# Laying the false arms of two run-time tests next in the program of an attention and expert kernel

## The chip, the core and the metric

The kernel runs on one core of a Trainium2 chip. The metric is the device time of one execution in microseconds (us). Each of the core's engines has a program of its own: TensorE (PE; its weight loads are shown apart as PEld), VectorE (DVE), ScalarE (ACT), GpSimd (POOL) and SyncE (SP), the last of which here does nothing but start transfers and read numbers into registers. They meet through semaphores. A run-time test stands in all five programs: each engine reads the number into a register of its own and branches by itself.

## The reference, cut to what matters

Three stages follow each other on 1536 tokens of width 512: attention with a local window and block summaries, a dense layer of three weight matrices with a maximum, and an expert layer. Only the last matters here:

```
skip_score = x @ w_skip
do_compute = skip_score > 0
out = x.copy()
xc = x[do_compute]
logits = xc @ w_gate
e_idx = np.argmax(logits, axis=1)
... gate_w: the softmax probability of the chosen expert
for e in range(E):                       # 8 experts
    mask = e_idx == e
    h = np.maximum(xc[mask] @ w1[e], 0.0)
    y[mask] = gate_w[mask, None] * (h @ w2[e])
out[do_compute] = xc + y
```

How many tokens go to which expert is known only when the program runs, so the number of token tiles (128 tokens each) per expert is a number in a register, and the program branches on it.

## The kernel before, in words

The attention stage and the dense layer are one long straight program, written out by hand-made planning (`arrange`), and fill the first 297 us. While they end, the counts of tokens per expert are taken (`guess`, `plan`), and written as small integers to the tile `ints`. Matrix products are made of three TensorE passes each, on a high and a low part of either factor (the `h` and `l` in `wh`, `wl`, `xth`, `xtl`).

The expert stage then goes through token tiles. `pair(p, t)` works on two tiles (256 tokens) of the expert whose weights lie in buffer set p: `first(f)` multiplies into `ph` banks (L1111), ACT and DVE make `hth` and `htl` of it (L1114, L1115), `second(f)` multiplies into `py` (L1123, shown as pm), and `end(2)` adds and scatters the rows to `out` (DVE L1086, POOL L1089). In the middle, `next_x` prepares `xth`, `xtl` for the next pair (ACT L738, DVE L739). `single(p, t)` works on one tile: its first products are at L1204, the Relu at L1206, the turning of the hidden values at L1210 to L1212, the second products at L1246. With `dense=True` it works on the last 128 rows of the whole token list in their place, reads those rows of `out` back (SP, L1181), does its last products at L1176 in two halves, and writes the rows (DVE L1185, SP L1186).

`pair` and `single` begin with `begin`: POOL copies the indices and the rows of the tiles (L1070, L1072). Nothing that PE does in its first products reads them; DVE's last addition does.

The order of the expert stage is set by nested tests. After two pairs a test at L1349 (others to do than the common case) leads to `most`, and there:

- two pairs more, then L1325: are there more than 5 tiles left for the biggest expert? If so, another pair, then
- L1327: more than 7? If so, yet another pair. Then `odd()`, which is written out in each arm:
- L1319: is the count odd? If so a single tile. Then `last()`, written out in each arm again:
- L1311: is there a `DENSE` mark? If so, `single` for the second expert and `single` with `dense=True`.

With the inputs here the test of L1325 holds, L1327 and L1319 do not, and L1311 does: the profile shows five pairs (40 ACT instructions of L1114, 8 for each pair), then one single tile and the dense one. So one arm of each of the four tests is run, and the program ends.

Where an arm lies in the program is a matter of its own. `preferred_fallthrough_block=True` puts the true arm right behind the test and the false arm far away; `False` puts the false arm right behind it. Without the argument the true arm lies next. The arm that lies far away is reached by a jump, in all five programs.

Of the kernel before, what the change touches and what calls it, by code (L numbers as in the profile page):

```python
# [43 lines left out]
ONES, DENSE, OTHER = 32, 64, 128  # L44
# [102 lines left out]
def build(tc, a, out):  # L147
# [571 lines left out]
    def reg(t, hi, **kw):  # L719
        return nc.values_load(t, min_val=0, max_val=hi, skip_runtime_bounds_check_because=why, **kw)  # L720
# [34 lines left out]
    def raw_load(c, e):  # L755
        nc.sync.dma_start(M2["raw"][c], chunk_src(c, e))
# [110 lines left out]
    for n, (j, f) in enumerate(ws):  # L867
        t, w = 19.7 + 4.25 * n, (j, f)
# [8 lines left out]
    for f in range(FT1):  # L877
        t, w = 24.7 + 4.25 * ws.index((3, f)), (3, f)
# [143 lines left out]
    def tail_i(row):  # L1022
        nc.sync.dma_start(mi, table[bass.ds(row, TAIL), :].unsqueeze(0).broadcast_to([4, TAIL, 2]))
# [275 lines left out]
    def most(w):  # L1299

        b0, b1, l0 = (reg(ints[:, i * NE + k:i * NE + k + 1], 14, **SP) for i, k in ((2, 0), (2, 1), (3, 0)))
        MR[1], MR[2] = (reg(ints[:, 5 * NE + k:5 * NE + k + 1], NROW - P, **SP) for k in (1, 2))
        e2 = reg(ints[:, NE + 2:NE + 3], NE - 1, **SP)
        pair(0, b0 + 1, 1)
        tail_i(MR[2])
        for c in range(NCH):
            raw_load(c, e2)
        pair(0, b0 + 2, FAST2)

        def last():  # L1310
            with tc.If((w & DENSE) > 0, preferred_fallthrough_block=True) as dense:  # L1311
                single(1, b1 + 1, last=True, hr=M2["raw"], then=True)
                single(0, 0, last=True, hr=M2["raw"][2:], dense=True)
            with dense.Else():
                with tc.If((w & ONES) > 0):
                    single(1, b1 + 1, last=True, hr=M2["raw"])

        def odd():
            with tc.If((w & 1) > 0) as one:  # L1319
                single(0, l0, hr=M2["raw"])  # L1320
                last()
            with one.Else():
                last()

        with tc.If((w & (ONES - 1)) > 5, preferred_fallthrough_block=True) as four:  # L1325
            pair(0, b0 + 3)
            with tc.If((w & (ONES - 1)) > 7, preferred_fallthrough_block=True) as five:  # L1327
                pair(0, b0 + 4)
                odd()
            with five.Else():  # L1330
                odd()
        with four.Else():
            odd()
# [9 lines left out]
    with tc.If(EA > EARLY, preferred_fallthrough_block=True) as early2:  # L1343
        with tc.manual_schedule():
            pair(0, 0, gen=steps())
            numbers()
            pair(0, 1)
            word = reg(ints[:, 6 * NE:], 2 * OTHER - 1)
            with tc.If(word >= OTHER, preferred_fallthrough_block=False) as others:  # L1349
                any_ranks()  # L1350
            with others.Else():
                most(word)
# [78 lines left out]
```

## Time and profile before

| what | us |
|---|---|
| median of three runs (460.86 to 462.88) | 462.82 |
| the profiled execution, its own time | 464.36 |
| its span, from first to last instruction | 462.6 |
| PE busy in the span | 434.4 (94%) |
| DVE, ACT, POOL busy | 248.8, 197.6, 127.9 |
| attention and dense layer | 0 to 297 |
| five pairs | 297 to 423.6 |
| single tile, dense tile, end | 423.6 to 462.6 |

To be read so: a busy PE is the engine that sets the pace nearly everywhere, and a stretch in which it stands still is time of the whole kernel unless another engine is late as well. "issue" in a wait or in the chain of waits is time in which an engine waited for nothing that the profile shows. [...]

### The profile page before, as it was taken

Reading aid. Unit: us, or ns where it says so; the run is one execution under the profiler, and the core shown is the slowest. Engines: PE = TensorE matmul, PEld = TensorE weight load, DVE = VectorE, ACT = ScalarE, POOL = GpSimd, SP = SyncE. Lnnn points to the kernel's source line nnn. Section 1 sums busy time; section 2 is a strip of 40 time slices with the busy share of each in tenths; the row PEclk is TensorE's granted clock in tenths of the full one; section 3 lists DMA queues with packets and bytes.
Section 4 is the critical chain, followed back from the end, with each engine's and each line's share of the span. In section 5 each row is a group of like instructions: output and inputs, shape, how many; then the busy total and the mean of one; then the engine's idle time right before and its main releaser. Section 6 shows DMA issues by size and latency. Waiting matters only on the chain.

```text
span 462.6 us, 9488 instructions
## 1 busy us (share of the span) xinstructions
PE 434.4 (94%) x3446; PEld 390.4 (84%) x3450; DVE 248.8 (54%) x787; ACT 197.6 (43%) x522; POOL 127.9 (28%) x177
## 2 busy tenths in 40 slices
PE   7977979999999999999999999999999999996895
PEld 3556769999999899989999988998999798895775
DVE  4887999989963353445114174587147631313021
ACT  2799987755464482356211173211116412111111
POOL 2232453233112440433102511142323123322100
PEclk9998989999999999999999999999999999999799
DMA  8993644567525265220030290312941570011001
GB/s 237 256 303 112 221 151 143 183 228 233 201 84 189 93 182 132 39 86 27 3 117 21 52 350 12 137 10 82 331 129 46 169 264 27 28 48 28 28 28 50
DMA packets 28173, 58.51 MB, mean 126 GB/s; under 512 B 6163, under 2 KB 8723, under 8 KB 28104
## 3 DMA queue, kind: packets, MB, share of 16 engines
q1 hardware_dynamic: 25544, 51.71, 35.3%
q0 software_dynamic: 2560, 5.96, 4.1%
q8 instruction: 33, 0.54, 0.5%
q14 instruction: 36, 0.29, 0.2%
HBM read 48.16 MB, written 10.47 MB: 127 GB/s over the span
## 4 chain that ended last, share of the span: by engine, by line
PE 70%; DVE 9%; DMA 6%; issue 5%; ACT 5%; POOL 2%; SPq 1%; POOLq 0%; ACTq 0%
PE pm L368 19%; PE ph L1111 13%; PE pm L1123 12%; PE pm L395 11%; PE ph L1204 3%; ACT pr L278 3%; DMA raw<-in_m 3%; DMA raw<-in_kt 2%; PE pt L293 2%; PE po L306 2%; PE sc L259 2%; DVE cx L349 1%; PE pm L1176 1%; PE ptx L731 1%; DVE cx L353 1%
## 5 line engine op out<-in xcount | busy, mean ns | idle before, releaser
L368 PE MATMUL pm<-xh,wh 128*128 128x384 f32 x288 | 67.0, 352 | 2.5 <-DVE t L377 1.3
L368 PE MATMUL pm<-xl,wh 128*128 128x384 f32 x288 | 62.8, 337 | 0.0
L368 PE MATMUL pm<-xh,wl 128*128 128x384 f32 x288 | 62.6, 336 | 0.0
L368 PEld LDWEIGHTS pm<-xh,wh 128*128 128x128 f32 x288 | 50.3, 192 | 4.8 <-DVE t L377 1.9
L1114 ACT ACTIVATE hth<-ph 128x256 fp32r<-128x256 f32 x40 | 15.4, 386 | 88.8 <-PE ph L1111 85.5
L368 PEld LDWEIGHTS pm<-xl,wh 128*128 128x128 f32 x288 | 51.8, 189 | 0.0
L368 PEld LDWEIGHTS pm<-xh,wl 128*128 128x128 f32 x288 | 51.3, 188 | 0.3 <-DVE wl L361 0.3
L1115 DVE SCALAR_TENSOR_TENSOR htl<-ph,hth 128x256 fp32r<-128x256 f32 x40 | 16.8, 422 | 57.1 <-ACT hth L1114 57.1
L377 DVE TENSOR_TENSOR t<-pm,t 128x384 f32<-128x384 f32 x48 | 26.5, 553 | 37.8 <-PE pm L368 36.9
L288 POOL TENSOR_TENSOR pr<-pr,se 128x360 f32<-128x360 f32 x32 | 26.2, 824 | 68.9 <-DVE se L284 48.0
L395 PE MATMUL pm<-wh,h 128*128 128x262 f32 (+1 forms) x288 | 42.7, 287 | 1.3 <-ACT v L215 1.1
L278 ACT ACTIVATE pr<-pr,mx 128x120 f32<-128x120 f32 x96 | 36.7, 386 | 10.6 <-DVE mx L272 10.5
L385 POOL TENSOR_TENSOR h<-t,h 128x384 fp32r<-128x384 f32 x24 | 26.1, 1093 | 49.1 <-ACT h L382 47.6
L395 PEld LDWEIGHTS pm<-wh,h 128*128 128x128 f32 x288 | 37.9, 189 | 2.1 <-ACT v L215 1.3
L1123 PE MATMUL pm<-wh,hth 128*128 128x512 f32 x80 | 31.8, 397 | 0.0
L1123 PE MATMUL pm<-wh,htl 128*128 128x512 f32 x80 | 31.4, 393 | 0.0
L1123 PE MATMUL pm<-wl,hth 128*128 128x512 f32 x80 | 31.3, 392 | 0.0
L343 POOL TENSOR_SCALAR cx<-cx 128x512 f32<-128x512 f32 x24 | 18.3, 762 | 37.0 <-ACT cx L335 33.3
L562 POOL DMA_INDIRECT table<-rtab,rsi x12 | 12.0, 997 | 59.7 <-DVE rsi L553 25.3
L744 POOL DMA_INDIRECT xn<-x2d,inx x14 | 14.9, 1065 | 46.8 <-DVE xm L1077 31.1
L382 ACT CAST h<-t 128x384 fp32r<-128x384 f32 x24 | 11.9, 513 | 35.2 <-DVE t L377 33.8
L1111 PE MATMUL ph<-xth,wh 128*128 128x256 f32 x160 | 26.4, 286 | 0.0
(342 smaller groups left out, 871.2 us busy)
## 6 DMA issues: line engine op xcount, KB each, us to landing
raw<-in_m SPq DMA_DIRECT2D x48, 256.0 KB, 4.7
raw<-in_wx SPq DMA_DIRECT2D x22, 512.0 KB, 4.3
kx<-in_kx SPq DMA_DIRECT2D x12, 360.0 KB, 3.8
vx<-in_vx SPq DMA_DIRECT2D x14, 288.0 KB, 3.8
qt<-in_qt SPq DMA_DIRECT2D x16, 192.0 KB, 5.8
x2d<-raw SPq DMA_DIRECT2D x12, 256.0 KB, 4.7
raw<-in_kt SPq DMA_DIRECT2D x7, 384.0 KB, 9.4
raw<-in_vt SPq DMA_DIRECT2D x7, 384.0 KB, 5.0
```

Of the source, the lines that this page charges most:

```text
L278: nc.scalar.activation(pr[:, t, :], pr[:, t, :], AF.Exp, bias=mx[:, t:t + 1], scale=-1.0, accum_out=se[:, t:t + 1])
L288: nc.gpsimd.tensor_tensor(pr, pr, se.unsqueeze(2).broadcast_to([P, TPG, KT]), ALU.mult)
L343: nc.gpsimd.tensor_scalar(x, x, HIGH, LOW, ALU.min, ALU.max)
L368: nc.tensor.matmul(ST["ch", u, f, j], l[j, f][:, c * P:(c + 1) * P], r[u][:, c, :], start=(cs[0] == 0 and n == 0), stop=(cs[-1] == KC1 - 1 ...
L377: nc.vector.tensor_tensor(ST["t1", u, f], ps, ST["t1", u, f], ALU.max)
L385: nc.gpsimd.tensor_tensor(HL[u, f], ST["t1", u, f], HH[u, f].bitcast(F32), ALU.subtract)
L395: nc.tensor.matmul(ps, l[u, f][:, t * P:(t + 1) * P], r[3, f][:, lo:hi], start=(part != 1 and n == 0), stop=(part != 0 and n == len(ops) - 1))
L744: nc.gpsimd.indirect_dma_start(out=xn[t], out_offset=None, in_=x2d, in_offset=bass.IndirectOffsetOnAxis(ap=inx[:, t, 0:1], axis=0), bounds ...
L1111: nc.tensor.matmul(ps, w[:, o:o + P], r[:, d, :], start=(n == 0), stop=(n == 3 * KC1 - 1))
L1114: nc.scalar.activation(hh, ps, AF.Relu)
L1115: nc.vector.scalar_tensor_tensor(hl, ps, 0.0, hh.bitcast(F32), ALU.max, ALU.subtract)
L1123: nc.tensor.matmul(py[i], l[:, o:o + P], r, start=(f == 0 and n == 0), stop=(f == 7 and n == 2))
```

## The change

Two tests in `most` get the argument that lays their false arms right behind them. No instruction is added or removed on any engine, and no wait: the two far arms and the two near ones change their places.

```
         def odd():
-            with tc.If((w & 1) > 0) as one:
+            with tc.If((w & 1) > 0, preferred_fallthrough_block=False) as one:
                 single(0, l0, hr=M2["raw"])
                 last()
             with one.Else():
...
             pair(0, b0 + 3)
-            with tc.If((w & (ONES - 1)) > 7, preferred_fallthrough_block=True) as five:
+            with tc.If((w & (ONES - 1)) > 7, preferred_fallthrough_block=False) as five:
                 pair(0, b0 + 4)
                 odd()
             with five.Else():
```

On PE, in the program before, the test of L1327 stands behind the last product of the fifth pair, and behind the test lies a sixth pair:

```order
L1123 MATMUL pm_4026<-wl0_5_3718,hth1_4022 128x512
L1123 MATMUL pm_4026<-wh0_5_3717,htl1_4024 128x512
L1327 REGISTER_ALU
L1327 COMPARE_AND_BRANCH
L1111 MATMUL ph0_3500<-xth_3509,wh0_0_3564 128x256
L1111 MATMUL ph0_3500<-xth_3509,wh2_0_3574 128x256
```

The false arm of it, the test of L1319, is about 10,000 rows further on, behind the arms for all other cases; behind that test lies a single tile, and the arm that is run, with the test of L1311, lies 236 rows behind it:

```order
L1315 UNCONDITIONAL_BRANCH x2
L1319 REGISTER_ALU
L1319 COMPARE_AND_BRANCH
L1204 MATMUL ph0_3500<-wh0_0_3564,xth_3509 128x512
L1204 MATMUL ph0_3500<-wl0_0_3565,xth_3509 128x512
...
L1311 REGISTER_ALU
L1311 COMPARE_AND_BRANCH
L1204 MATMUL ph0_3500<-wh1_5_3952,xth_3509 128x512
L1204 MATMUL ph0_3500<-wl1_5_3953,xth_3509 128x512
```

So two jumps are taken, at L1327 and at L1319, and none at L1311. On PE, in the program now, the three tests and the arm that is run stand in one piece:

```order
L1123 MATMUL pm_4026<-wl0_5_3718,hth1_4022 128x512
L1123 MATMUL pm_4026<-wh0_5_3717,htl1_4024 128x512
L1327 REGISTER_ALU
L1327 COMPARE_AND_BRANCH
L1319 REGISTER_ALU
L1319 COMPARE_AND_BRANCH
L1311 REGISTER_ALU
L1311 COMPARE_AND_BRANCH
L1204 MATMUL ph0_3500<-wh1_5_3952,xth_3509 128x512
L1204 MATMUL ph0_3500<-wl1_5_3953,xth_3509 128x512
L1204 MATMUL ph0_3500<-wh1_5_3952,xtl_3510 128x512
```

The product on `wh1_5` that came last in the far arm is now the third test's neighbour, and the sixth pair has gone to the far end. The programs of DVE, ACT, POOL and SP move in the same way. The jump from the end of the arm to the end of the program is there in both.

## Rows read from the trace of the kernel before

**Rows 1.** Page, busy time: us (share of the span) and instructions of each engine.

```profile
PE 434.4 (94%) x3446; PEld 390.4 (84%) x3450; DVE 248.8 (54%) x787; ACT 197.6 (43%) x522; POOL 127.9 (28%) x177
```

**Rows 2.** Chain of waits from 415 us on: start us, us, what.

```profile
423.65 5.58 issue
429.23 6.39 PE ph L1204 x18
```

**Rows 3.** Timeline, PE: start us, us, engine line, operation, tiles, count, [idle before].

```profile
423.26 0.39 PE L1123 MATMUL pm<-wh,htl 128*128 128x512 f32 x1
429.23 0.76 PE L1204 MATMUL ph<-wh,xth 128*128 128x512 f32 x1 [5.58 <-issue]
...
435.46 0.60 PE L1210 MATMUL ph<-ident,raw 128*128 128x128 f32 x4
```

**Rows 4.** Timeline, PE, the dense tile: the same eighteen products and turning.

```profile
444.75 0.39 PE L1204 MATMUL ph<-wh,xth 128*128 128x512 f32 x1
...
448.97 0.60 PE L1210 MATMUL ph<-ident,raw 128*128 128x128 f32 x4
```

**Rows 5.** Windows, PE: from:to and length us, busy (instructions), granted clock, DMA share, GB/s.

```profile
296.00:423.60 127.60, 127.59 (x967) 1.00 0.35 110
425.00:426.00 1.00, 0.00 (x0) 1.00 0.09 16
427.00:428.00 1.00, 0.00 (x0) 0.50 0.09 20
431.00:433.20 2.20, 2.20 (x6) 0.50 0.33 123
434.00:437.40 3.40, 3.40 (x18) 1.00 0.01 2
```

**Rows 6.** DMA queues, 423.6 to 426 us: packets, MB, share.

```profile
q8 instruction: 2, 0.03, 7.8%
```

**Rows 7.** Waits, 422 to 463 us: us in total, times, longest.

```profile
POOL ic L1070 <- issue: 4.0, 1, 4.0
```

**Rows 8.** Timeline around the tests of L1349 (344 us) and L1325 (400 us, POOL 408 us).

```profile
343.93 0.39 PE L1123 MATMUL pm<-wh,htl 128*128 128x512 f32 x1
344.16 0.66 PE L1111 MATMUL ph<-xth,wh 128*128 128x256 f32 x4
...
399.97 0.53 PEld L1111 LDWEIGHTS ph<-xth,wh 128*128 128x128 f32 x4 [0.20 <-issue]
...
407.33 0.97 POOL L1089 DMA_INDIRECT out<-yo,isc  x1 [2.56 <-DMA out<-yo,isc]
...
408.30 0.20 POOL L1070 COPY ic<-im 128x4 int32<-128x4 int32 x1
```

**Rows 9.** Timeline, DVE and POOL from 421 us on.

```profile
421.02 1.28 DVE L739 TENSOR_TENSOR xtl<-ptx,xth 128x512 fp32r<-128x512 f32 x2
423.01 1.43 DVE L1086 SCALAR_TENSOR_TENSOR yo<-pm,ic,xr 128x512 f32<-128x512 f32 x2 [0.70 <-PE pm L1123]
424.56 1.04 POOL L1089 DMA_INDIRECT out<-yo,isc  x1 [0.37 <-POOL isc L1087]
429.58 1.00 POOL L1089 DMA_INDIRECT out<-yo,isc  x1 [3.97 <-DMA out<-yo,isc]
434.68 0.61 POOL L1072 COPY xr<-xm 128x512 f32<-128x512 f32 x1
445.01 0.75 DVE L1086 SCALAR_TENSOR_TENSOR yo<-pm,ic,xr 128x512 f32<-128x512 f32 x1 [2.88 <-PE pm L1246]
446.58 0.99 POOL L1089 DMA_INDIRECT out<-yo,isc  x1 [11.16 <-DVE yo L1086]
```

**Rows 10.** Timeline, the end: SP's transfers and DVE's addition before the last.

```profile
449.45 0.35 SPq L1181 DMA_DIRECT2D xr<-out  x1
...
455.78 0.48 DVE L1185 SCALAR_TENSOR_TENSOR yo<-pm,mo,xr 128x256 f32<-128x256 f32 x1 [1.56 <-PE pm L1176]
...
457.72 0.34 SPq L1186 DMA_DIRECT2D out<-yo  x1
```

More of the change, by code (lines that the diff above doesn't have):

```diff
@@ L1318, in odd @@
         def odd():
-            with tc.If((w & 1) > 0) as one:
+            with tc.If((w & 1) > 0, preferred_fallthrough_block=False) as one:
                 single(0, l0, hr=M2["raw"])
@@ L1326, in most @@
             pair(0, b0 + 3)
-            with tc.If((w & (ONES - 1)) > 7, preferred_fallthrough_block=True) as five:
+            with tc.If((w & (ONES - 1)) > 7, preferred_fallthrough_block=False) as five:
                 pair(0, b0 + 4)
```

## The prediction, made before the changed kernel was run

> **What bounds the kernel now.** I read the page's busy times first: PE works in 94% of the span [rows 1], so the question is where the other 6% lie and whether one of them is at a test. The chain of waits answers it. It runs along PE from the fifth pair into the single tile, and between them stands one piece of 5.58 us that belongs to nobody: "issue", time in which PE waited for no other engine and no transfer that the trace shows [rows 2]. The timeline of PE shows the same hole from the other side: the last product of the fifth pair starts at 423.26, the first of the single tile at 429.23 [rows 3]. These two stand on either side of the tests of L1327 and L1319, which are both false here and both jump. In the hole, two packets of a queue that carries instructions move, 0.03 MB [rows 6], so PE's program itself was being brought in. POOL, which passes the same tests later, shows a hole of its own of 4.0 us right there [rows 7].
>
> The second thing to see is the clock. It is 1.00 through the pairs, still 1.00 at 425 to 426, and 0.50 at 427 to 428, after PE has stood still for some 3 us; the products that follow run at 0.50 until about 433.4, and at 434 it is 1.00 again [rows 5]. So the hole costs twice: while PE stands, and in the first products behind it.
>
> **The change, part by part.** Nothing is added to any engine's work. Two taken jumps become two that are not taken, on five engines. What matters is PE.
>
> 1. The hole. Within the fifth pair and in the dense tile one 512-wide product follows the other by 0.23 us: eighteen products from 444.75 to the turning at 448.97 take 4.22 us, 0.234 each [rows 4]. Without jumps the first product of the single tile would start 0.23 after 423.26, at 423.49. It started at 429.23. This is 5.74 us.
>
> 2. The clock. From the first product of the single tile to its first turning, the same eighteen products take 435.46 - 429.23 = 6.23 us [rows 3], where the dense tile takes 4.22 at clock 1.00 [rows 4]. The excess is 2.01 us. If PE never stands, the clock has no cause to fall: at clock 1.00 the pairs ran without a pause, 127.59 us of 127.6 [rows 5]. I count all of it as gained.
>
> 3. What tests cost that do not jump. Before already shows two such: L1349, whose false arm lies next, and L1325, whose true arm does. At L1349 the next product starts 0.23 us after the one before, as if there were no test; at L1325, which follows 64 short products, the weight load stands idle for 0.20 us; on POOL the next instruction after L1325 starts at 408.30, where the one before ends [rows 8]. The three tests now stand together on PE. Their cost lies between nothing (the seam of L1349, which like this one follows long products, behind which PE's program can run ahead) and 3 x 0.20 = 0.60 us. I take nothing, from the nearest row, and keep 0.6 for the range. It cannot be below nothing, since the same three tests are passed before.
>
> [...]
>
> 4. What could be late next. The single tile's first products need `xth` and `xtl`; DVE has made the latter at 421.02 + 1.28 = 422.30, 1.2 us before 423.49. The second products write the bank that DVE's addition reads until 424.44 [rows 9], and come 4.22 us and more behind the first, after 427.7. DVE's addition at the end of the single tile, at 445.01, would come 7.75 us earlier, at 437.26. It needs the rows that POOL copies until 434.68 + 0.61 = 435.29: already early enough by 2.0 us if POOL gained nothing, and POOL's own hole of 4.0 us goes as well. The scatter of the single tile, at 446.58, would come at 438.83; POOL has its predecessor off at 430.58, and the longest time that a scatter made the next wait here is 429.58 - 424.56 = 5.02 us, so it is free by 434.6 [rows 9]. The rows that SP reads back at 449.45 are needed by DVE at 455.78 [rows 10]; both move with the scatter and with PE, by the same amount. So the holes of DVE, ACT, POOL and SP are covered and worth nothing, and PE's are worth all.
>
> 5. The end. After SP's last transfer is issued at 457.72 + 0.34 = 458.06 [rows 10], the span goes on to 462.6. The jump to the program's end is in both programs, far away in both. I count no change.
>
> The sum: 5.74 + 2.01 = 7.75 us, less 0 to 0.6. The profiled execution's own time is 464.36, so it would be 456.61; that execution is 1.54 us over the median of the runs, 462.82. Against the median: 462.82 - 7.75 = 455.07, taken as 455.1.
>
> **The rivals.**
>
> One stall stays. The hole is the price of two jumps; I do not know from the trace how it divides. If code behind three tests in a row, or the first stretch of the new arm, is still brought in late once, PE would stand for half the hole, 5.74 / 2 = 2.87 us. That is shorter than the 3 us or so after which the clock fell, so the second gain stays whole: 7.75 - 2.87 = 4.88, or 457.9. For it: instruction packets move in the hole, so fetching is slow enough to be seen. Against it: PE ran from 296 to 423.6 through two such tests and four seams between pairs without a stall [rows 5, 8].
>
> Nothing changes. Either the hole is not the price of the jumps but of testing (three tests, 1.9 us each, taken or not), or the places in the program do not survive to the chip. Then 462.8. Against it: two tests that are not taken show 0 and 0.20 us [rows 8].
>
> PE without a rest loses its clock: the slower side. In the program before, the pause at 423.65 is the one rest PE has between 296 us and the end. If the clock were then lowered later, at the dense tile, its products from 444.75 to about 457.2, 12.4 us at 1.00, would take twice that. The price is 12.4 us at most, and it decides from 7.75 us of lost time on; in full it gives 462.82 - 7.75 + 12.4 = 467.5. Against it: 127.6 us of unbroken work with the clock at 1.00 go before, and the one fall of it in this stretch came after PE had stood still, not after it had worked [rows 5].
>
> **How the numbers follow.** Full gain 0.80, its own range 453.4 to 456.6 (0.6 for the tests, and some 1.5 us either way for the spread of 2.0 us that the three runs of before show). One stall stays 0.12 (457.9). Nothing changes 0.05 (462.8). The clock is lost later 0.03 (467.5). The likeliest is 455.1. A range from 453.3 to 458.3 holds nearly all of the first two cases and leaves out the others. Faster by over 0.5% (2.3 us, about what a measurement of this kernel can tell from no change) are the first two cases: 0.92. Same 0.05, slower 0.03.
>
> **What would show it.** In the profile after: no piece "issue" of more than 0.6 us in the chain at the fifth pair's end; the first product of L1204 less than 1 us behind the last of L1123; granted clock 1.00 from there to the end of the dense tile; eighteen products to the first turning in 4.2 us; POOL's hole before L1070 gone; all from 429 on earlier by 7 to 8 us, with an end as long as before, some 4.5 us behind SP's last issue. A hole of 2 to 4 us at the same place with the clock at 1.00 would show that one stall stays. I would be wrong if PE reached the single tile early and then stood there for POOL, or if the clock were 0.50 anywhere behind 423 us.

## The result, and the profile after

The changed kernel takes 456.09 us (median of six runs, 454.20 to 456.77). The kernel before takes 462.15 (six runs, 460.86 to 466.73). The ratio is 0.985, with a 95% interval of 0.981 to 0.990, so between 4.6 and 8.9 us were gained. The prediction had 455.1 and a range from 453.3 to 458.3. The profiled execution of the changed kernel has an own time of 456.73 and a span of 454.8; that of before had 464.36 and 462.6. These differ by 7.63 us.

The chain of waits of the changed kernel, through the place of the change and on to the end (start us, us, what), answers to [rows 2]:

```profile
419.60 4.09 PE pm L1123 x18
423.69 4.20 PE ph L1204 x18
427.89 0.44 PE ph L1210 x4
...
445.07 4.30 PE pm L1176 x36
449.37 0.02 issue
449.39 0.48 DVE yo L1185
```

The piece of 5.58 us that belonged to nobody is gone: PE goes from the eighteen last products of the fifth pair straight into the eighteen first of the dense arm's single tile. The timeline of PE in the changed kernel (start us, us, engine line, operation) answers to [rows 3]:

```profile
423.30 0.39 PE L1123 MATMUL pm<-wh,htl 128*128 128x512 f32 x1
423.53 0.39 PE L1204 MATMUL ph<-wh,xth 128*128 128x512 f32 x1
...
427.73 0.60 PE L1210 MATMUL ph<-ident,raw 128*128 128x128 f32 x4
```

From the last product before the tests to the first behind them it is 0.23 us, where it was 5.97. From there to the turning (L1210) it is 4.20 us, where it was 6.23. The windows of PE in the changed kernel (from:to and length us, busy, granted clock as a share of full speed, DMA share, GB/s) answer to [rows 5]:

```profile
296.00:423.40 127.40, 127.40 (x971) 1.00 0.34 111
423.40:429.00 5.60, 5.60 (x28) 1.00 0.13 47
429.00:441.00 12.00, 11.55 (x56) 1.00 0.12 45
441.00:449.50 8.50, 8.35 (x64) 1.00 0.13 42
```

The clock stays at 1.00 to the end of PE's work. It is simplest to measure the tail: from the start of the last product before the tests (423.26 before, 423.30 now) to the end of the span. It was 39.34 us and is 31.50, so 7.84 less: 5.74 for the hole, 2.03 for the clock, and 0.07 for all the rest. The stretch ahead of it has the same instructions in both kernels, and it is not equally long in every execution: in the profiles below the last product before the tests starts anywhere between 418.4 and 424.9 us. This is why I go by the tail below, which two profiles of the changed kernel repeat to about 0.1 us (31.50 here, 31.61 below), and use the medians only for what they can tell.

POOL in the changed kernel, the timeline, answers to [rows 7]; its hole ahead of L1070 has gone as well:

```profile
428.19 1.00 POOL L1089 DMA_INDIRECT out<-yo,isc  x1 [2.55 <-DMA out<-yo,isc]
429.17 0.21 POOL L1070 COPY ic<-im 128x4 int32<-128x4 int32 x1
```

### The profile page after: what moved, and what is told of

Its sections match the earlier page's. It is cut to its first block, busy times and chain, and to the rows that moved or that the text cites. A ratio compares the mean times of both kernels' runs of the same rounds, so it can differ in the third digit from the quotient of the medians.

```text
span 454.8 us, 9492 instructions
## 1 busy us (share of the span) xinstructions
PE 433.1 (95%) x3450; PEld 390.4 (86%) x3450; DVE 247.6 (54%) x787; ACT 197.5 (43%) x522; POOL 127.4 (28%) x177
## 4 chain that ended last, share of the span: by engine, by line
PE 71%; DVE 8%; DMA 8%; ACT 4%; issue 4%; POOL 2%; SPq 1%; POOLq 0%; ACTq 0%; DVEq 0%
PE pm L368 22%; PE ph L1111 13%; PE pm L1123 12%; PE pm L395 9%; DMA kx<-in_kx 3%; DMA raw<-in_m 3%; PE ph L1204 2%; ACT pr L278 2%; PE po L306 2%; PE pt L293 2%; PE sc L259 2%; DVE cx L349 1%; PE pm L1176 1%; DVE cx L353 1%; DMA raw<-in_vt 1%
## 5 line engine op out<-in xcount | busy, mean ns | idle before, releaser
L1123 PE MATMUL pm<-wh,hth 128*128 128x512 f32 x80 | 31.7, 397 | 0.0
L1123 PE MATMUL pm<-wh,htl 128*128 128x512 f32 x80 | 31.4, 393 | 0.0
L1123 PE MATMUL pm<-wl,hth 128*128 128x512 f32 x80 | 31.3, 392 | 0.0
```

The costliest lines, as they stand in the source:

```text
L1123: nc.tensor.matmul(py[i], l[:, o:o + P], r, start=(f == 0 and n == 0), stop=(f == 7 and n == 2))
```

## The experiments

The prediction left open how the hole divides between its two jumps. **Theory A**, the prediction's own rival, gives each jump half of it, 2.87 us. **Theory B** says that the first jump pays all. **Theory C** says that part of the price is that of testing. **Theory D** came up with the first results; it says that PE's program runs ahead of its products (is read and passed on while earlier products still wait to be done), so that the first jump is reached, and its fetch begun, while products are still at work. Below, the seam is always the time from the start of the last product of L1123 to that of the first of L1204; without any hole it is 0.23 us.

**The changed kernel once more** (both_false_next), in the runs of the next three.

> The changed kernel again, beside the others. Theory A (the hole is the price of jumping far, shared out over the two jumps) and theory B (the first far jump pays all of it) both expect 7.75 us less than before, ratio about 0.983, and no hole at the end of the fifth pair.

Measured: ratio 0.981 (0.978 to 0.985), median 454.25. The seam is 0.23, the eighteen products 4.20 and the tail 31.61, as in the first profile.

**One edit alone** (five_only and odd_only).

```
 five_only: with tc.If((w & 1) > 0) as one:                                                    # as before
            with tc.If((w & (ONES - 1)) > 7, preferred_fallthrough_block=False) as five:       # as changed
 odd_only:  with tc.If((w & 1) > 0, preferred_fallthrough_block=False) as one:                 # as changed
            with tc.If((w & (ONES - 1)) > 7, preferred_fallthrough_block=True) as five:        # as before
```

> Only the false arm of the test for a fifth pair (L1327) lies next; the test for an odd count (L1319) still jumps far. Theory A: half the hole stays, 2.9 us, too short for the clock to fall, so 4.9 us less than before (ratio 0.989). Theory B, one far jump costs the whole hole: 5.6 us of issue and the clock at 0.50 behind it, so the time of before (ratio 1.00). Theory C, that testing costs and not jumping: as the kernel before.

> Only the false arm of the test for an odd count (L1319) lies next; the test for a fifth pair (L1327) still jumps far, to a place where the tests of L1319 and L1311 and the arm that is run follow each other. Theory A: half the hole, 2.9 us, 4.9 us less than before (ratio 0.989). Theory B: the whole hole and the fallen clock, the time of before (ratio 1.00). If the second of the two jumps is the dear one: no hole here, as with both, ratio 0.983.

Measured: ratios of 0.984 (0.980 to 0.988) and 0.983 (0.979 to 0.988). Either edit alone brings most of the gain. The chain of waits of five_only:

```profile
415.86 4.09 PE pm L1123 x18
419.94 1.01 issue
420.95 4.43 PE ph L1204 x18
```

and of odd_only:

```profile
416.95 4.09 PE pm L1123 x18
421.04 1.45 issue
422.48 4.44 PE ph L1204 x18
```

One far jump costs 1.16 us in five_only (the seam of 1.39 less 0.23) and 1.60 in odd_only (1.83 less 0.23), and the clock holds: the eighteen products to the turning take 4.27 and 4.28. Theories A and B both fall, since the two alone make 2.76 us together and the two in a row 5.74. POOL's hole ahead of L1070 is there with one jump too; five_only, timeline of POOL:

```profile
429.99 0.18 POOL L1070 COPY ic<-im 128x4 int32<-128x4 int32 x1 [4.04 <-issue]
```

It is as long as before [rows 7] and costs nothing that can be seen: that kernel's tail, 32.84, is 1.34 us over the changed kernel's 31.50, and PE's seam and its eighteen products alone account for 1.16 and 0.07 of it; the 0.11 left is what the same kernel's tail differs by.

Where the rest of the first jump's price goes shows in an instruction queue, q8, which I take to be the one that brings in PE's program (the runs that hold back PE alone, below, move its packet along). In the kernel before, between 421.5 and 422 us (packets, MB, share of 16 engines):

```profile
q8 instruction: 1, 0.02, 11.8%
```

and in odd_only between 419.5 and 420:

```profile
q8 instruction: 1, 0.02, 12.7%
```

The products go on until 423.65 in the one and until 421.04 in the other. The packet moves 1.5 to 2 us before PE falls idle, which is how theory D came up.

**No tests at all behind the fifth pair** (no_tests). The arms for other inputs are left out.

```
-            with tc.If((w & (ONES - 1)) > 7, preferred_fallthrough_block=False) as five:
-                pair(0, b0 + 4)
-                odd()
-            with five.Else():
-                odd()
+            single(1, b1 + 1, last=True, hr=M2["raw"], then=True)
+            single(0, 0, last=True, hr=M2["raw"][2:], dense=True)
```

> The changed kernel without the tests of L1327, L1319 and L1311 in this arm: the single and the dense tile follow the fifth pair at once (the cases of other inputs are left out). If tests that don't jump cost nothing on PE: as with both false arms next, within 0.3 us (ratio 0.983 of before), the first product of the single tile 0.23 us behind the last of the pair. If three tests cost up to 0.6 us: that much less.

Measured: ratio 0.982 (0.978 to 0.986), seam 0.23, tail 31.43 against 31.50 and 31.61 with the tests. Three tests that do not jump cost PE nothing that can be seen here, where its program is ahead of its products; theory C falls.

**A hole without a jump** (hole_by_wait): the changed kernel, and ahead of `odd()` in the false arm eleven copies on DVE and a turning on PE that waits for the last of them.

```
             with five.Else():
+                for _ in range(11):
+                    nc.vector.tensor_copy(xr[1], xm[1])
+                nc.tensor.transpose(ptx[1][:, :P], xr[1][:, :P], ident)
                 odd()
```

> Both false arms next, no jump, but PE is made to wait: eleven copies of 128x512 on DVE into a buffer of no further use, and one turning of it on PE ahead of the single tile. DVE is free at about 424.5 and takes some 0.4 us for each, so PE should stand for some 5 us. If the clock falls after 3 us of standing and costs as before: hole 5 and the first 18 products 6.2 instead of 4.2 us, in all 7 us slower than with both (ratio to before about 0.997). If the slow products of the kernel before came from the jump and not from standing: only the 5 us (ratio 0.993).

Measured: ratio 1.003 (1.000 to 1.006), so this takes away all of the gain. The timeline of PE:

```profile
429.24 0.45 PE L1333 MATMUL ptx<-ident,xr 128*128 128x128 f32 x1 [6.95 <-DVE xr L1332]
429.81 0.77 PE L1204 MATMUL ph<-wh,xth 128*128 128x512 f32 x1
...
435.29 0.60 PE L1210 MATMUL ph<-ident,raw 128*128 128x128 f32 x4
```

and the windows of PE:

```profile
425.00:426.00 1.00, 0.00 (x0) 0.83 0.47 180
426.00:427.00 1.00, 0.00 (x0) 0.50 0.00 0
429.20:433.00 3.80, 3.64 (x10) 0.57 0.00 0
433.00:434.00 1.00, 1.00 (x6) 1.00 0.00 0
```

PE stands from 422.29 on, for DVE and for no code: no packet of an instruction queue moves between 422 and 430. The standing, 6.95 us, came out longer than the 5 or so that were expected. The clock falls all the same, and the eighteen products take 5.48 us, 1.28 over 4.20. The second term of the prediction's sum therefore belongs to the standing still and not to the jump. Its price was smaller here than the 2.03 of before, after a longer hole.

**A jump over very little, and one over a pair** (near_jump and near_pair): the changed kernel with one more test in the false arm, whose own arm is not run here and lies next, so that it is jumped over.

```
             with five.Else():
+                with tc.If((w & 1) > 0, preferred_fallthrough_block=True):
+                    nc.vector.memset(yq[:1], 1.0)      # near_jump
+                    pair(0, b0 + 4)                    # near_pair, in its place
                 odd()
```

> Both false arms next, and one more test in the path whose true arm (one small fill on DVE) lies next and is jumped over: one taken jump of one to three rows. If a jump costs by bringing in code that isn't there: no hole on PE, time as with both (ratio 0.981 to 0.984). If every taken jump costs what one far jump cost (a hole of 1.0 to 1.45 us on PE): 1 to 1.5 us slower than with both.

> As the near jump, but a whole pair (154 products on PE) lies between the test and its target. If the code behind the test has been brought in that far ahead, no hole; if not, the hole of a far jump, 1.0 to 1.45 us. No theory of this study says which; it tells how near is near.

Measured: ratios of 0.981 (0.977 to 0.986) and 0.985 (0.980 to 0.990). The timeline of PE in near_jump:

```profile
423.08 0.39 PE L1123 MATMUL pm<-wh,htl 128*128 128x512 f32 x1
423.31 0.39 PE L1204 MATMUL ph<-wh,xth 128*128 128x512 f32 x1
```

and in near_pair:

```profile
422.58 0.39 PE L1123 MATMUL pm<-wh,htl 128*128 128x512 f32 x1
423.96 0.47 PE L1204 MATMUL ph<-wh,xth 128*128 128x512 f32 x1 [0.99 <-DVEq L1331]
```

One more test costs PE nothing (0.23 again). With the jump over a pair (154 rows on PE) there is a hole of 0.99 us, and the trace puts it down to DVE's sequencer at the end of the inserted test; DVE's addition ends at 423.76, 0.20 before PE starts. But a packet of q8 moves at 421.2 as well, 2.7 us ahead of PE's first product, as one does 2.8 us ahead of it in five_only. Either could be the cause, so this run doesn't tell what the jump itself costs. I call it inconclusive.

**Three jumps in a row** (three_jumps): the kernel before, with the false arm of L1311 next as well, so that this test, too, is jumped from.

```
-            with tc.If((w & DENSE) > 0, preferred_fallthrough_block=True) as dense:
+            with tc.If((w & DENSE) > 0, preferred_fallthrough_block=False) as dense:
```

> The kernel before, with the arm of L1311 that is run laid far as well, so three far jumps follow each other. Theory D: PE's program runs some 3 us ahead of its products, so the first jump is nearly hidden (hole 1.0 to 1.45), and each further one costs its full fetch, about 4 us: hole about 9.5, 4 us slower than before (ratio 1.009). Theory E: two jumps were dear only because the second fell together with a scatter's transfer: a third adds at most 1.5 us (ratio 1.003).

Measured: ratio 1.000 (0.997 to 1.004). The timeline of PE:

```profile
420.98 0.39 PE L1123 MATMUL pm<-wh,htl 128*128 128x512 f32 x1
427.34 0.77 PE L1204 MATMUL ph<-wh,xth 128*128 128x512 f32 x1 [5.97 <-issue]
...
434.33 0.60 PE L1210 MATMUL ph<-ident,raw 128*128 128x128 f32 x4
```

and its windows:

```profile
425.00:426.00 1.00, 0.00 (x0) 1.00 0.08 25
426.00:427.30 1.30, 0.00 (x0) 0.70 0.01 3
427.30:434.00 6.70, 6.66 (x17) 0.55 0.14 49
```

The third jump costs 0.39 us (a seam of 6.36 after 5.97), where theory D as I had put it asked for about 4. Theory E, which allowed a third jump at most 1.5 us, is not refuted by this run; the runs that hold PE, below, bear on it. The arm that the third jump goes over is only 62 rows long on PE, against 236 for L1319's, and it brings in nothing of its own: three packets of q8 move ahead of the first product here (at 419.3, 422.7 and 423.1), as many as in the kernel before (421.6, 424.7 and 425.1). So a jump is not dear for being taken: this one cost 0.39 us, where the one of L1319, with which two packets move, cost 4.14 in the kernel before (below). What decides whether code has to be brought in for a jump, no run here shows.

**Holding PE's program at the pair's end** (wait_both, wait_odd, wait_near_pair). A turning that waits for DVE's last addition of the pair is put ahead of the tests. PE can't start on the tests early, and if theory D holds, a far jump then shows its whole price. Theory F says that one far jump costs 1.2 to 1.6 us whatever stands ahead of it.

```
             pair(0, b0 + 3)
+            nc.tensor.transpose(ptx[1][:, :P], yo[1][:, :P], ident)     # wait_both: on the changed kernel
             with tc.If((w & (ONES - 1)) > 7, ...) as five:              # wait_odd: True, so the false arm is far
                 ...                                                     # wait_near_pair: near_pair's test beside it
```

> Both false arms next, and PE held at the end of the fifth pair, before the test of L1327: one turning of the rows that DVE adds last. PE cannot run ahead of its products past it. No jump, so all theories expect only the wait: the first product of the single tile some 1.5 us behind the last of the pair instead of 0.23, about 1.3 us slower than with both (ratio to before about 0.986).

> The same hold, and one far jump behind it (L1327, as in the run with the odd test alone). Theory D, that PE's program reaches the jump 2 to 3 us ahead of its products and hides that much of the fetch: nothing is hidden now, so the first product of the single tile comes 3.5 to 4.5 us later than with the hold alone, and the clock may fall. Theory F, that one far jump costs 1.2 to 1.6 us whatever stands before: 1.2 to 1.6 us later than with the hold alone.

> The same hold, and behind it no far jump but one over a pair (154 products). If that jump needs a fetch as a far one does (its hole was 1.2 us without the hold): the same 3.5 to 4.5 us behind the hold alone. If the code behind the pair was there already: as the hold alone.

Measured: ratios of 0.985 (0.980 to 0.991), 1.000 (0.997 to 1.003) and 0.989 (0.984 to 0.993). The timeline of PE in wait_both, with no jump:

```profile
423.50 0.33 PE L1327 MATMUL ptx<-ident,yo 128*128 128x128 f32 x1 [0.85 <-DVE yo L1086]
424.30 0.48 PE L1204 MATMUL ph<-wh,xth 128*128 128x512 f32 x1 [0.48 <-issue]
```

and in wait_odd, with one:

```profile
422.59 0.33 PE L1327 MATMUL ptx<-ident,yo 128*128 128x128 f32 x1 [0.84 <-DVE yo L1086]
427.08 0.77 PE L1204 MATMUL ph<-wh,xth 128*128 128x512 f32 x1 [4.15 <-issue]
...
433.58 0.60 PE L1210 MATMUL ph<-ident,raw 128*128 128x128 f32 x4
```

The hold alone cost more than expected: the seam is 2.04 (some 1.5 expected), and the tail of wait_both, 33.44, is 1.94 over the changed kernel's. In it are 0.48 us of issue between the turning and the first product, where the three tests lie; whether that is their price once PE's program is not ahead, no run here tells. From the turning to the first product it is 0.80 without a jump and 4.49 with it: the far jump costs 3.69 us when nothing covers it, where odd_only paid 1.60 for the same jump. PE's instruction packet now moves between 423.5 and 424 us, behind the turning and no longer ahead of PE's standing still:

```profile
q8 instruction: 1, 0.02, 15.4%
```

PE now stands for 4.15 us at the jump, and the clock falls as well; windows of PE in wait_odd:

```profile
424.00:426.00 2.00, 0.00 (x0) 0.79 0.36 135
426.00:427.00 1.00, 0.00 (x0) 0.50 0.00 0
```

The eighteen products take 6.50, 2.22 over the 4.28 of wait_both. One jump with its cover taken away costs 3.69 + 2.22; with the 1.94 of the hold that is 7.85, the whole gain of the changed kernel lost again, and the median says the same (462.38, beside 462.58 for the kernel before). Theory D holds and F falls: 2.09 us of this jump (3.69 less 1.60) lie beside the pair's last products in odd_only. The hold also moves the fetch beside a scatter's transfer (theory E): the mean DMA share from packet to first product is 0.24 in wait_odd and 0.07 in odd_only. But from the packet to the first product it is 3.3 us in the one and 2.9 in the other, so at most some 0.4 of the 2.09 can come from that.

In wait_near_pair, PE's timeline and two of its windows:

```profile
426.08 0.33 PE L1327 MATMUL ptx<-ident,yo 128*128 128x128 f32 x1 [0.84 <-DVEq L1332]
427.45 0.47 PE L1204 MATMUL ph<-wh,xth 128*128 128x512 f32 x1 [1.04 <-PEq L1332]
```

```profile
427.00:428.00 1.00, 0.55 (x3) 1.00 0.34 119
430.00:431.00 1.00, 1.00 (x4) 0.50 0.00 0
```

The first product comes 1.37 us behind the turning, 0.57 later than in wait_both, and no packet of PE's instruction queue moves between the two. So the jump over a pair brought in no code ahead of that product in this run (a packet moves only at 427.5, behind its start); 0.57 is what it and its test cost together here at the most. The clock fell although PE had stood only for 0.84 and for 1.04 us. The profiled execution, 462.2, is the longest of this kernel's five, whose median is 458.1; whether the clock falls in the others isn't known.

**A straight program** (straight): every test from the first pair on is left out, with all the arms for other inputs, so that the last jump to the program's end goes too.

```
+    with tc.manual_schedule():
+        pair(0, 0, gen=steps())
+        numbers()
+        pair(0, 1)
...
+        pair(0, b0 + 3)
+        single(1, b1 + 1, last=True, hr=M2["raw"], then=True)
+        single(0, 0, last=True, hr=M2["raw"][2:], dense=True)
```

> The path that is run, from the first pair to the program's end, without any test and without the last jump (the cases of other inputs are left out). If the last jump is hidden behind the last transfer: as with both false arms next, ratio 0.981 to 0.985, and 4.5 us from SP's last issue to the end of the span. If the last jump is exposed on SP: the end shorter by 1 to 3 us, ratio 0.976 to 0.981.

Measured: ratio 0.977 (0.972 to 0.982), median 452.14. The seam is 0.23. The last transfer that SP issues in the changed kernel:

```profile
448.48 1.76 SPq L1186 DMA_DIRECT2D out<-yo  x2
```

and in straight:

```profile
445.69 1.77 SPq L1186 DMA_DIRECT2D out<-yo  x2
```

From the end of it to that of the span (454.8 and 449.9) it is 4.56 us in the first and 2.44 in the second. In this stretch five packets of the two instruction queues move in the changed kernel and one in straight. So the jump to the program's end, with what it brings in, stands bare behind the last work and is worth some 2.1 us; it is in the kernel before as well as after. The run leaves out every other test and arm too, but up to SP's last transfer this changes nothing: from the first turning to it, it is 22.5 and 22.6 us. This is no version to use, as it can serve no other inputs. One that keeps every arm and has the common one run into the end of the program wasn't tried; of those tried that keep every arm, none is measurably better than the changed kernel.

## Why the prediction was right

**The hole** (5.74 predicted, 5.74 measured). Both numbers, and both of the clock below, take the excess from the same profile of the kernel before, so their agreement to 0.02 us proves little by itself; what was at stake is that nothing of either stays, and nothing did. The step was sound because it used only the distance between products on either side, not the division of the hole. In the changed kernel the seam is the 0.23 us of any two products.

**The clock** (2.01 predicted, 2.03 measured in the tail). The cause was right: hole_by_wait shows the fall with no jump at all, and the changed kernel, whose PE does not stand, keeps 1.00. But this price is that of one execution. For a hole of some 3.7 to 7 us the excess over the kernel's own eighteen products without a fall was 1.28 (hole_by_wait), 2.03 (before), 2.22 (wait_odd) and 2.79 (three_jumps, 6.99 less 4.20). A range of some 1.3 to 2.8 for this term would have been fairer than a single number.

**The tests** (nothing taken, 0.6 kept for the range). Nothing was right: 0.23 with three tests, with four in near_jump, and with none in no_tests. The row of L1349 was the right one to read, as products of 512 columns stand ahead there as well, and the 0.20 us at L1325 did not return. That is with products still ahead of the tests; in wait_both, where PE is held in front of them, 0.48 us of issue stand there, and whether they are the price of testing was not shown.

**What is late next** (nothing). The chain after has no issue piece above 0.04 us between the tests and DVE's last addition; it passes over ACT and DVE once, from 431.56 to 433.13, 1.57 us as before. POOL's copy ends at 429.93, and DVE's addition in the single tile, predicted at 437.26, starts at 437.21.

**The end** (no change). It was 4.54 us and is 4.56.

**The rivals.** "One stall stays" did not come about. Its price, half the hole for each jump, was wrong as well: one jump that stays costs 1.16 or 1.60 us, because its fetch starts 1.5 to 2.0 us before PE falls idle, and only a second one in a row costs 4.14 (5.74 less the 1.60 of the first alone). As a case of "one edit does not take" it would have given a gain of over 6 us, not of 4.88. The reason that it put at the centre, that the clock would not fall behind one stall, held in both runs (1.01 and 1.45 us of issue, the eighteen products in 4.27 and 4.28), and failed once the stall had no cover (4.15 us in wait_odd, clock 0.50). "Nothing changes" and "PE without rest loses its clock" are refuted by the seam and by the windows of after, at 1.00 to the end.

**The time.** 7.75 was predicted off the median shown; the tail says 7.84, and the two ratios, 0.985 and 0.981, are worth 6.7 and 8.7 of 462. I put the difference between these two down to the first 420 us, which no edit touches and which differ between profiles by up to 6.5 us; for the runs without a profile this is not shown. The measured 456.09 is 1.0 over the 455.1 predicted. The prediction's own range for the full gain, 453.4 to 456.6, leaves its 0.6 us for tests out at the upper end (455.07 + 0.6 + 1.5 is 457.2); as the tests cost nothing, this did no harm.

What stays open: the second far jump in a row cost 4.14 us in the kernel before, and a single one without cover 3.69. A scatter's transfer runs beside both (a mean DMA share of 0.24 from the packet to the first product in either), so it does not explain the 0.45 us between them. The second jump's fetch moves two packets (424.7 and 425.1) and that of wait_odd one; whether this or another property of the target makes the difference, no run tells.

## What to carry to other kernels

At a run-time test, lay the arm that is usually run next, and look in the chain of waits for "issue" pieces on the engine that sets the pace: they can be code being brought in (here 5.58 us, with two packets of q8 inside), and packets of an instruction queue in or just ahead of the piece speak for it. Count the far jumps that follow each other: the first is partly covered by the products that are still queued ahead of it (it cost 1.2 to 1.6 us here), a second, or one behind a wait, cost its full 3.7 to 4.1 us, and on top of it came 2.0 to 2.8 us of slow clock. Since the two do not add up, one of two edits can bring most of the gain (here 0.984 and 0.983 alone, 0.981 together), and a test that does not jump cost nothing on PE where PE's program was ahead of its products.

## What the runs showed of the hardware that was not expected

- PE's program ran about 2 us ahead of its products here (the packet for the jump moved 1.5 to 2.0 us before PE fell idle), and most of what it did in that time, a jump's fetch too, was free: up to 2.09 us of 3.69 in odd_only.
- What PE did before its clock fell differed much: in three_jumps it had stood still since 421.37 and the clock was still 1.00 between 425 and 426, while in wait_near_pair rests of 0.84 and 1.04 us with a turning between them went ahead of a fall. The "3 us or so" of the prediction is not a constant.
- In near_pair, at a test without an else arm, the trace names DVE's sequencer for 0.99 us of PE. What lies behind it is not shown, as a packet of q8 moves 2.7 us ahead of PE's product there too; in near_jump, whose test has the same form, PE waited for nobody (0.23 from product to product).
- The jump from the last arm to the program's end cost about 2.1 us here (4.56 against 2.44 behind SP's last transfer), at a place where nothing covers it.
